# A fused attention and two-layer kernel on one core: the first group's attention with VectorE, ScalarE and GpSimd in program order

## The chip, the core and the metric

The kernel runs on one core of a Trainium2 chip. The time is device microseconds of that core for one execution of the whole program. In the rows, PE is TensorE (PEld its weight loads), DVE is VectorE, ACT is ScalarE, POOL is GpSimd and SP is the engine that issues nearly all transfers.

## What is computed

Block-causal attention over 4 batches, 8 heads, 576 tokens of 64 numbers, then two feed-forward layers on the 2304 token rows. Cut to what matters:

```
scores = (q @ k^T) / 8, keys of later 64-blocks masked
attn   = exp(scores - max) ; attn /= sum(attn) + 1e-9
x      = attn @ v                      # 2304 x 512
h = x @ w_in ; x = (h - tanh(h)) @ w_out                 # 512 -> 2048 -> 512
xn = x / rms(x) * g ; out = (silu(xn @ w_gate) * (xn @ w_val)) @ w_out2
```

All inputs are float32 (float64 words for the weights, which the kernel reads as pairs of 32-bit words and converts itself).

## The kernel before

**Tiling.** Attention runs over units: a unit is one batch with either its first 384 queries or its last 192. Four pairs of heads make one unit. The units in turn fill six groups of 384 token rows, and group g of the first layer (`w_in`, `tanh`, `w_out`) runs on TensorE while the attention of later groups is done beside it. The first group (batch 0, queries 0 to 383) has nothing to run beside: until its attention is done, TensorE has only attention work. This is the stretch from 8 to 41 us, and the change touches nothing else. Six score tiles belong to a pair in it, with 64, 128, 192, 256, 320 and 384 keys; the first three are called the first half here, the other three the second half. P1 to P4 are the pairs of the first group, P5 and P6 the first two of the second.

**One pair.** Its keys and queries are transposed on TensorE (L235; L242 from P5 on), and copied out of PSUM: keys by ScalarE to `kh`, queries by VectorE to `qf` in two copies of 64 partitions (of P1 the second is ScalarE's). Each score tile is a product on TensorE (L481), which VectorE reads out while it finds the row's extreme (L494), and ScalarE turns into exponentials with their sum (L496). GpSimd clears the padding (L499). After a half, ScalarE adds 1e-9 to the three sums (L504, tile `stat`), VectorE takes the reciprocals (L505), and GpSimd scales the three tiles by them (L510). TensorE then transposes the scaled tiles (L525); the six transposes are copied to `pp`, in this group 1, 3, 4 and 6 by VectorE (copy 1, 3, 4, 6 below), 2 and 5 by ScalarE. Twelve products with the values (L577) end the pair; ScalarE rounds the result to `xh` and VectorE subtracts to `xl`.

**The order on TensorE** is written out: `plan` lists scores ("s"), transposes ("t") and the product with the values ("a") by half-pairs, so that a half's transposes come two halves after its scores, and the "a" of a pair stands between the first-half scores and the first-half transposes of later pairs. So while the scores of P3 are read, P2's tiles are transposed and P1's values are multiplied. All score, transpose and product tiles of this stretch use eight PSUM banks in turn.

**Weight conversions.** `conv_upto` spreads four conversions of weight blocks over the first group. One takes two ScalarE passes over the loaded words (`cv`, `cu`), then two VectorE steps that clamp and join them (L144, L145); where the block is also split in two parts, a ScalarE rounding (`w<-cv`) and a VectorE subtraction follow. Conversions 1 and 3 (`w_in` blocks) are split, 2 and 4 are not.

**The order on the others.** Only TensorE's order is that of the program (L592). On VectorE, ScalarE and GpSimd the framework's scheduler places the instructions by its own estimate of times; each engine then runs its list in that order and waits at an instruction until its inputs are there.

## Time and profile before

| | us |
|---|---|
| median of 3 runs (lowest, highest) | 1019.18 (1018.07, 1019.55) |
| profiled execution | 1019.15 |
| its span, first to last instruction | 1017.4 |
| PE busy in the span | 1001.5 |
| DVE, ACT, POOL busy in the span | 704.4, 660.2, 347.4 |
| 8.00 to 41.04 us (first group's attention): PE, DVE, ACT, POOL busy | 31.56, 29.72, 27.77, 19.32 of 33.04 |
| 41.04 to 60.00 us: PE, DVE, ACT, POOL busy | 18.33, 16.19, 17.76, 7.12 of 18.96 |
| 60.00 to 120.00 us: PE, DVE, ACT, POOL busy | 58.83, 44.48, 50.35, 11.11 of 60.00 |

The 1.75 us between span and execution lie outside the instructions. Busy times of PE are modelled ends of pipelined products, so small gaps hide in them; starts of neighbouring rows tell more. For an engine that runs its list in order, the time from one row's start to the next row's start is what a row costs it.

### The profile page before, as it was taken

The page shows a single profiled execution, that of the slowest core. Times are in us where ns is not written, and L with a number is a line of the kernel's source. Part 1 is how long each engine was busy: PE and PEld are TensorE (multiplying, and loading weights), DVE is VectorE, ACT ScalarE, POOL GpSimd, SP SyncE. Part 2 cuts the span into 40 slices and gives each one's busy share as a digit, 9 for nine tenths or more (in the row PEclk, how much of TensorE's full clock was granted, in tenths as well). Part 3 has the DMA queues.
Part 4 walks back from the last instruction along what each step waited for, and adds up shares of the span by engine and source line. Part 5 has one row for each costly group of instructions (what it writes and reads, how often), then busy time and mean ns, then how long its engine had stood idle before and what let it go on. Part 6 is the DMA issues. An engine that isn't in the chain of part 4 may idle for free.

```text
span 1017.4 us, 17824 instructions
## 1 busy us (share of the span) xinstructions
PE 1001.5 (98%) x5983; PEld 921.6 (91%) x5983; DVE 704.4 (69%) x1497; ACT 660.2 (65%) x1530; POOL 347.4 (34%) x474
## 2 busy tenths in 40 slices
PE   8999999999999999999999999899999999999998
PEld 5766789999999999999899889899999999999998
DVE  6877867876777677787757887866854558644465
ACT  6978978887888777787857775635732247412253
POOL 6522112322233342434334425575121470112610
PEclk9999999999999999999999999999999999999999
DMA  9899959965798689867879997986796757876664
GB/s 236 250 342 340 283 173 258 272 205 140 197 254 206 187 248 271 234 215 240 279 225 377 363 364 299 322 336 265 284 333 256 252 224 265 303 270 239 248 235 139
DMA packets 185419, 265.22 MB, mean 261 GB/s; under 512 B 109040, under 2 KB 150384, under 8 KB 178032
## 3 DMA queue, kind: packets, MB, share of 16 engines
q1 hardware_dynamic: 184384, 263.83, 79.2%
q8 instruction: 47, 0.77, 0.3%
q10 hardware_dynamic: 944, 0.26, 0.1%
q14 instruction: 44, 0.36, 0.1%
HBM read 201.65 MB, written 62.39 MB: 260 GB/s over the span
## 4 chain that ended last, share of the span: by engine, by line
PE 80%; DVE 5%; ACT 4%; issue 1%; POOL 1%; DVEq 0%; ACTq 0%; POOLq 0%
PE gv L1064 5%; PE t L715 5%; PE t L481 5%; PE gv L1062 5%; PE gv L1063 5%; PE t L717 5%; PE t L716 5%; PE acc L748 5%; PE acc L750 5%; PE acc L749 4%; PE t L525 3%; PE ga L1064 3%; PE ga L1063 3%; PE ga L1062 3%; PE ga L748 3%; PE ga L750 2%
## 5 line engine op out<-in xcount | busy, mean ns | idle before, releaser
L715 PE MATMUL t<-xh,w 128*128 128x384 f32 x384 | 138.6, 361 | 0.1
L717 PE MATMUL t<-xh,w 128*128 128x384 f32 x384 | 129.9, 338 | 0.4 <-DVE w L108 0.2
L716 PE MATMUL t<-xl,w 128*128 128x384 f32 x384 | 129.2, 337 | 0.0
L1064 PE MATMUL gv<-xh,ws 128*128 128x384 f32 x322 | 108.5, 337 | 3.6 <-DVE ws L108 3.6
L1062 PE MATMUL gv<-xh,ws 128*128 128x384 f32 x322 | 108.3, 336 | 0.2 <-DVE vb L1115 0.2
L1063 PE MATMUL gv<-xl,ws 128*128 128x384 f32 x322 | 108.0, 336 | 0.0
L748 PE MATMUL acc<-w,gh 128*128 128x512 f32 x252 | 102.5, 407 | 0.0
L750 PE MATMUL acc<-w,gl 128*128 128x512 f32 x252 | 99.6, 395 | 0.4 <-DVE gl L108 0.3
L749 PE MATMUL acc<-w,gh 128*128 128x512 f32 x252 | 99.1, 393 | 0.0
L1119 POOL TENSOR_TENSOR g<-va,vb 128x384 f32<-128x384 f32 x36 | 40.5, 1126 | 150.9 <-ACT va L1118 150.9
L496 ACT ACTIVATE pt<-pt,stat 128x64 f32<-128x64 f32 (+2 forms) x144 | 80.0, 556 | 18.6 <-DVE pt L494 17.1
L494 DVE TENSOR_SCALAR_CACHE_REDUCE pt<-t 128x64 f32<-128x64 f32 (+2 forms) x144 | 63.8, 449 | 18.6 <-PE t L481 17.4
L715 PEld LDWEIGHTS t<-xh,w 128*128 128x128 f32 x384 | 72.3, 188 | 4.3 <-issue 1.5
L716 PEld LDWEIGHTS t<-xl,w 128*128 128x128 f32 x384 | 72.5, 189 | 2.3 <-issue 0.5
L717 PEld LDWEIGHTS t<-xh,w 128*128 128x128 f32 x384 | 72.1, 188 | 1.0 <-DVE w L108 1.0
L108 DVE TENSOR_TENSOR gl<-gt,gh 128x384 fp32r<-128x384 f32 x84 | 57.2, 681 | 16.4 <-ACT gh L103 16.1
L980 DVE TENSOR_TENSOR gt<-t,gt 128x384 f32<-128x384 f32 x84 | 46.2, 550 | 31.0 <-ACT gt L974 30.7
L108 DVE TENSOR_TENSOR pp<-t,pp 128x512 fp32r<-128x512 f32 (+3 forms) x112 | 55.3, 507 | 15.6 <-ACT pp L103 14.7
L525 PE MATMUL t<-ident,pt 128*128 128x128 f32 x400 | 64.4, 274 | 0.8 <-POOL pt L510 0.7
L1064 PEld LDWEIGHTS gv<-xh,ws 128*128 128x128 f32 x322 | 60.5, 188 | 4.5 <-DVE ws L108 4.5
L103 ACT ACTIVATE pp<-t 128x512 fp32r<-128x512 f32 (+5 forms) x144 | 60.2, 433 | 6.2 <-PE t L525 5.6
L525 PEld LDWEIGHTS t<-ident,pt 128*128 128x128 f32 x400 | 49.7, 140 | 14.1 <-issue 3.4
(188 smaller groups left out, 2960.0 us busy)
## 6 DMA issues: line engine op xcount, KB each, us to landing
ws<-w2d SPq DMA_DIRECT2D x26, 1792.0 KB, 7.9
ws<-wod SPq DMA_DIRECT2D x21, 1536.0 KB, 6.1
w<-w1d_i SPq DMA_DIRECT2D x60, 512.0 KB, 5.1
w<-w1d_o SPq DMA_DIRECT2D x48, 512.0 KB, 5.1
w2d<-ws SPq DMA_DIRECT2D x10, 1792.0 KB, 8.4
st<-in_moe_w_out SPq DMA_DIRECT2D x28, 512.0 KB, 5.9
st<-in_moe_w_in SPq DMA_DIRECT2D x16, 512.0 KB, 6.0
w1d_i<-w SPq DMA_DIRECT2D x16, 512.0 KB, 6.2
```

The lines of the kernel that those rows point to most:

```text
L108: eng.tensor_tensor(out=o, in0=full, in1=hi.bitcast(F32), op=ALU.subtract)
L496: ACT.activation(out=pt[:, 0:keys], in_=pt[:, 0:keys], func=AF.Exp, scale=-1.0, bias=least, accum_out=st[:, 8 + ti:9 + ti])
L525: PE.transpose(t[:, (j - a) * 128:(j - a + 1) * 128], pt[:, j * 128:(j + 1) * 128], ident)
L715: PE.matmul(h, lhsT=wh[:, c], rhs=xh[:, kk], start=(kk == 0), stop=False)
L716: PE.matmul(h, lhsT=wh[:, c], rhs=xl[:, kk], start=False, stop=False)
L717: PE.matmul(h, lhsT=wl[:, c], rhs=xh[:, kk], start=False, stop=(kk == KD - 1))
L748: PE.matmul(acc, lhsT=gh[:, c], rhs=wh, start=first, stop=False, skip_group_check=more)
L749: PE.matmul(acc, lhsT=gh[:, c], rhs=wl, start=False, stop=False, skip_group_check=more)
L750: PE.matmul(acc, lhsT=gl[:, c], rhs=wh, start=False, stop=last, skip_group_check=more)
L1062: PE.matmul(ps, lhsT=wh[:, c], rhs=xh[:, kk], start=(first and kk == 0), stop=False, skip_group_check=more)
L1063: PE.matmul(ps, lhsT=wh[:, c], rhs=xl[:, kk], start=False, stop=False, skip_group_check=more)
L1064: PE.matmul(ps, lhsT=wl[:, c], rhs=xh[:, kk], start=False, stop=(last and kk == nk - 1), skip_group_check=more)
```

## The change

For the first group alone, VectorE, ScalarE and GpSimd are put in the order in which the program is written, too, and the writing is changed to suit:

- The sums' addition, the reciprocals and the scaling (`norm`) are issued two steps of the list after their half's last score, not at once.
- A weight conversion is issued in four steps: the two ScalarE passes at once, clamp and join two steps later, rounding three, subtraction four steps later; the store of the block follows the last.
- The GpSimd reorders of P5's to P8's keys and queries (`kt`, `qt`) are issued behind the first half's scores of the pair two ahead of them.
- In the list itself all three transposes of a second half now stand behind all three scores (before, the first of them stood ahead of the third score).
- P1's two query copies, one on VectorE and one on ScalarE, are declared independent.

The core of the diff:

```diff
@@ q1, the query copies @@
-            for hh in range(2):
-                rnd(DVE if u.light and (hh == 0 or u.group or p) else ACT, diag(d["q"][0], hh, TG), part(ps, hh, TG))
+            engs = (DVE, DVE if u.group or p else ACT) if u.light else (ACT, ACT)
+            copies = [rnd(engs[hh], diag(d["q"][0], hh, TG), part(ps, hh, TG)) for hh in range(2)]
+            if engs[0] is not engs[1]:
+                tc.declare_no_dep(copies[1].ins, copies[0].ins, reason="they write different partitions")
@@ convert @@
-        pin(DVE.tensor_scalar(f, f, HIGHEST * REBIAS, -HIGHEST * REBIAS * NEGATIVE, ALU.min, ALU.max))
-        DVE.scalar_tensor_tensor(h.bitcast(I32) if l is None else t, t, 3, u, ALU.logical_shift_left, ALU.bitwise_or)
-        if l is None:
-            return
-        rnd(ACT, h, f)
-        lo(DVE, l, f, h)
+
+        def join():
+            pin(DVE.tensor_scalar(f, f, HIGHEST * REBIAS, -HIGHEST * REBIAS * NEGATIVE, ALU.min, ALU.max))
+            DVE.scalar_tensor_tensor(h.bitcast(I32) if l is None else t, t, 3, u, ALU.logical_shift_left, ALU.bitwise_or)
+        defer(2, join)
+        if l is not None:
+            defer(3, lambda: rnd(ACT, h, f))
+            defer(4, lambda: lo(DVE, l, f, h))
@@ plan @@
-                if av and self.pairs[av[0][1]][0].group == 0:
+                if any(self.pairs[e[0][1]][0].group == 0 for e in (av, tr) if e):
                     self.seq += sc + av + tr
@@ Attn @@
+        def defer(self, n, f):
+
+            if self.inorder:
+                self.waiting.append([n, f])
+            else:
+                f()
...
         def step(self):
+            self.tick()
@@ scores @@
             if ti % 3 < 2:
                 return
+            if self.inorder and ti == 2 and i + 2 in self.loads:
+                rows_in_turn(self.pairs[i + 2][0], self.loads[i + 2])
+            self.defer(2, lambda: self.norm(u, d, ti))
+
+        def norm(self, u, d, ti):
+            st = d["st"]
             r = st[:, 16 + ti - 2:17 + ti]
             ACT.activation(out=r, in_=st[:, 8 + ti - 2:9 + ti], func=AF.Copy, bias=1e-9)
             DVE.reciprocal(r, r)
@@ convert1 @@
-                convert(staged.pop(n), t[:, 0:512], t[:, 512:1024])
+                convert(staged.pop(n), t[:, 0:512], t[:, 512:1024], att.defer)
...
-                    SP.dma_start(out=w1d[0][j], in_=t.bitcast(F32))
+                    att.defer(4, lambda: SP.dma_start(out=w1d[0][j], in_=t.bitcast(F32)))
@@ around the first group's loop @@
+        inorder = ExitStack()
+        inorder.enter_context(tc.manual_schedule(engines={DVE.engine, ACT.engine, POOL.engine}))
+        att.inorder = True
...
+        att.tick(True)
+        att.inorder = False
+        inorder.close()
```

`tick`, called at the head of every step, counts the waiting pieces down and issues those that are due.

What this makes of the engines' lists is shown at three places. The names are those of the code: `pt` with a number of columns is a score tile read out (VectorE) or turned into exponentials (ScalarE), `pp` a copied transpose, `qf` the query copies.

VectorE (DVE), from the third score of P4 to the fourth, before:

```order
L494 TENSOR_SCALAR pt,stat<-t 128x192
L144 TENSOR_SCALAR cv<-cv 128x512
L505 RECIPROCAL stat<-stat 128x3
L145 SCALAR_TENSOR_TENSOR w_485<-cv,cu 128x512
L105 COPY pp<-t 128x2x64
L105 COPY pp<-t 128x2x2x64
```

and now:

```order
L145 TENSOR_SCALAR cv<-cv 128x512
L146 SCALAR_TENSOR_TENSOR w_487<-cv,cu 128x512
L523 TENSOR_SCALAR pt,stat<-t 128x192
L107 TENSOR_TENSOR xl<-t,xh 128x384
L540 RECIPROCAL stat<-stat 128x3
L104 COPY pp<-t 128x2x64
L104 COPY pp<-t 128x2x2x64
```

The join of a conversion stands ahead of the 192-key score, and the subtraction `xl` and its reciprocal ahead of the copies and of the 256-key score; before, they stood behind that score.

VectorE, next in the list: the second half of P4 and the start of P5, before:

```order
L494 TENSOR_SCALAR pt,stat<-t 128x256
L108 TENSOR_TENSOR xl<-t,xh 128x384
L505 RECIPROCAL stat<-stat 128x3
L494 TENSOR_SCALAR pt,stat<-t 128x320
L105 COPY pp<-t 128x2x2x64
L494 TENSOR_SCALAR pt,stat<-t 128x384
L105 COPY pp<-t 128x3x2x64
L494 TENSOR_SCALAR pt,stat<-t 128x64
L494 TENSOR_SCALAR pt,stat<-t 128x128
L105 COPY qf_139<-t 64x6x64 x2
L505 RECIPROCAL stat<-stat 128x3
```

and now:

```order
L523 TENSOR_SCALAR pt,stat<-t 128x256
L523 TENSOR_SCALAR pt,stat<-t 128x320
L523 TENSOR_SCALAR pt,stat<-t 128x384
L104 COPY pp<-t 128x2x2x64
L540 RECIPROCAL stat<-stat 128x3
L104 COPY pp<-t 128x3x2x64
L523 TENSOR_SCALAR pt,stat<-t 128x64
L523 TENSOR_SCALAR pt,stat<-t 128x128
L104 COPY qf_139<-t 64x6x64 x2
L523 TENSOR_SCALAR pt,stat<-t 128x192
```

The second half's reciprocal stood behind P5's query copies; it now stands directly behind copy 4 and ahead of copy 6 and of all of P5's rows.

ScalarE (ACT), from P5's 128-key exponentials to its 256-key ones, before:

```order
L496 ACTIVATE pt,stat<-pt,stat 128x128
L496 ACTIVATE pt,stat<-pt,stat 128x192
L103 ACTIVATE xh<-t 128x384
L504 ACTIVATE stat<-stat 128x3
L141 ACTIVATE cv<-st 128x512
L143 ACTIVATE cu<-st 128x512
L103 ACTIVATE pp<-t 128x2x64
L496 ACTIVATE pt,stat<-pt,stat 128x256
```

and now:

```order
L525 ACTIVATE pt,stat<-pt,stat 128x128
L525 ACTIVATE pt,stat<-pt,stat 128x192
L140 ACTIVATE cv<-st 128x512
L142 ACTIVATE cu<-st 128x512
L103 ACTIVATE xh<-t 128x384
L539 ACTIVATE stat<-stat 128x3
L103 ACTIVATE w_615<-cv 128x512
L103 ACTIVATE pp<-t 128x2x64
L525 ACTIVATE pt,stat<-pt,stat 128x256
```

The two passes of conversion 3 stand ahead of `xh`, and the rounding `w` ahead of the 256-key exponentials; before, the passes stood behind `xh` and the rounding two rows behind those exponentials.

On GpSimd the two reorders of a pair stand behind the scaling of a second half instead of ahead of it. On SP the store of the first converted block goes ahead of one query load. Behind the first group the lists of all engines are nearly those of before.

## Rows read from the trace of the kernel before

**Rows 1.** windows, to the first group's end: length, busy us (instructions) of each engine, PEclk, DMA, GB/s

```profile
8.00:41.04 33.04, 31.56 (x213) 23.16 (x213) 29.72 (x115) 27.77 (x102) 19.32 (x49) 1.00 1.02 246
```

**Rows 2.** waits, first 50 us: engine, tile, line <- releaser: us in total, times, longest

```profile
PEld t L525 <- POOL pt L510: 3.0, 5, 1.0
```

**Rows 3.** timeline, PE: start, duration (us), line, operation, count [idle before <-releaser]

```profile
8.02 1.44 PE L481 MATMUL t<-kh,qf 128*128 128x64 f32 x8 [0.60 <-ACT qf L103]
...
30.12 0.33 PE L481 MATMUL t<-kh,qf 128*128 128x64 f32 x2
...
36.09 0.33 PE L481 MATMUL t<-kh,qf 128*128 128x64 f32 x2
...
37.81 0.44 PE L715 MATMUL t<-xh,w 128*128 128x384 f32 x1
...
39.59 1.52 PE L577 MATMUL t<-pp,vn 128*64 128x384 f32 x12
```

**Rows 4.** timeline, ACT, 0 to 75 us: first pair's second query copy

```profile
7.39 0.48 ACT L103 ACTIVATE qf<-t 64x384 f32<-64x384 f32 x1 [0.58 <-DVE qf L105]
```

**Rows 5.** timeline, DVE, 0 to 75 us: a reciprocal, then the fourth pair

```profile
15.63 0.18 DVE L505 RECIPROCAL stat<-stat 128x3 f32<-128x3 f32 x1 [0.52 <-ACT stat L504]
...
24.75 0.55 DVE L105 COPY pp<-t 128x384 f32<-128x384 f32 x1
25.22 0.20 DVE L494 TENSOR_SCALAR_CACHE_REDUCE pt<-t 128x64 f32<-128x64 f32 x1
...
26.71 0.36 DVE L494 TENSOR_SCALAR_CACHE_REDUCE pt<-t 128x192 f32<-128x192 f32 x1
...
27.45 0.69 DVE L145 SCALAR_TENSOR_TENSOR w<-cv,cu 128x512 int32<-128x512 int32 x1
28.07 0.61 DVE L105 COPY pp<-t 128x128 f32<-128x128 f32 x2
28.60 0.41 DVE L494 TENSOR_SCALAR_CACHE_REDUCE pt<-t 128x256 f32<-128x256 f32 x1
...
28.94 0.55 DVE L108 TENSOR_TENSOR xl<-t,xh 128x384 fp32r<-128x384 f32 x1
29.41 0.16 DVE L505 RECIPROCAL stat<-stat 128x3 f32<-128x3 f32 x1
29.49 0.46 DVE L494 TENSOR_SCALAR_CACHE_REDUCE pt<-t 128x320 f32<-128x320 f32 x1
```

**Rows 6.** timeline of all engines, 39.9 to 42.0 us: hand-overs between DVE and ACT

```profile
40.02 0.36 DVE L494 TENSOR_SCALAR_CACHE_REDUCE pt<-t 128x192 f32<-128x192 f32 x1
...
40.42 0.45 ACT L496 ACTIVATE pt<-pt,stat 128x192 f32<-128x192 f32 x1 [0.88 <-DVE pt L494]
...
40.99 0.20 ACT L504 ACTIVATE stat<-stat 128x3 f32<-128x3 f32 x1
...
41.16 0.49 ACT L103 ACTIVATE xh<-t 128x384 fp32r<-128x384 f32 x1
41.23 0.18 DVE L505 RECIPROCAL stat<-stat 128x3 f32<-128x3 f32 x1 [0.76 <-ACT stat L504]
...
41.68 0.56 DVE L108 TENSOR_TENSOR xl<-t,xh 128x384 fp32r<-128x384 f32 x1 [0.28 <-ACT xh L103]
```

**Rows 7.** timeline, ACT, 0 to 75 us: fourth pair

```profile
25.47 0.47 ACT L103 ACTIVATE kh<-t 128x384 f32<-128x384 f32 x1
25.84 0.67 ACT L141 ACTIVATE cv<-st 128x512 f32<-128x512 f32 x1
...
27.06 0.34 ACT L496 ACTIVATE pt<-pt,stat 128x64 f32<-128x64 f32 x1
...
29.05 0.51 ACT L496 ACTIVATE pt<-pt,stat 128x256 f32<-128x256 f32 x1
...
29.99 0.56 ACT L496 ACTIVATE pt<-pt,stat 128x320 f32<-128x320 f32 x1 [0.34 <-DVE pt L494]
...
30.92 0.60 ACT L496 ACTIVATE pt<-pt,stat 128x384 f32<-128x384 f32 x1
```

More of the change, by code (lines that the diff above doesn't have):

```diff
@@ L102, in rnd @@
         if eng is ACT:
-            ACT.activation(out=o, in_=i, func=AF.Copy)
-        else:
-            eng.tensor_copy(out=o, in_=i)
+            return ACT.activation(out=o, in_=i, func=AF.Copy)
+        return eng.tensor_copy(out=o, in_=i)
     def lo(eng, o, full, hi):
@@ L131, in stage, with convert @@
         return st
-    def convert(st, h, l=None):
+    def convert(st, h, l=None, defer=lambda n, f: f()):
         e = st.rearrange("p (e t) -> p e t", t=2)
@@ L291, in kq_loads, with rows_in_turn @@
         return d
+    def rows_in_turn(u, d):
+        if by_rows(u) and "kt" not in d:
+            d["kt"] = reorder("kt", d["kr"], POOL)
+            d["qt"] = reorder("qt", d["qr"], POOL)
     def v_loads(u, p, d):
         b, W = u.b, u.nk
-        if by_rows(u):
-            d["kt"] = reorder("kt", d["kr"], POOL)
-            d["qt"] = reorder("qt", d["qr"], POOL)
+        rows_in_turn(u, d)
         if u.group == 0:
@@ L364, in __init__ @@
             self.ready = set()
+            self.inorder = False
+            self.waiting = []
         def plan(self, units):
@@ L450, in prep, with tick @@
                     self.load()
+        def defer(self, n, f):
[3 more added lines that the diff above has]
+                f()
+        def tick(self, end=False):
+            while self.waiting:
+                now = []
+                for w in self.waiting:
+                    w[0] -= 1
+                    if w[0] <= 0 or end:
+                        now.append(w)
+                self.waiting = [w for w in self.waiting if w not in now]
+                for w in now:
+                    w[1]()
+                if not end:
+                    return
         def step(self):
+            self.tick()
             kind, i, t = self.seq[self.pos]
@@ L660, in convert1 @@
             o = t[:, 512 * (j % 2):512 * (j % 2) + 512]
-            convert(staged.pop(n), o)
+            convert(staged.pop(n), o, None, att.defer)
             wo[j] = o
             if j % 2:
-                SP.dma_start(out=w1f[j // 2], in_=t)
+                att.defer(2, lambda: SP.dma_start(out=w1f[j // 2], in_=t))
         fstaged = {}
```

## The prediction

> **What bounds the kernel now.** I read the busy times by stretch first. Between 8.00 and 41.04 us, the first group's attention, PE is busy for 31.56 of 33.04 us and DVE for 29.72 [rows 1]: TensorE has some 1.5 us without work there, VectorE 3.3 us. The granted clock is 1.00. So two engines are close to full, and neither has much to give. Next, the waits: TensorE's weight loads wait 3.0 us in the first 50 us for GpSimd's scaled tiles [rows 2]. That is what a change here can aim at. Then TensorE's timeline: from P5's first score to P6's first score is 30.12 to 36.09 us [rows 3], and TensorE works without a mark of idle time in these rows. I take 5.97 us as its own need for a pair. Last, VectorE's rows of P4 [rows 5]: they follow each other start to start, with a conversion between them, because the scheduler put ready work wherever a result of ScalarE was not yet there. The one wait among the rows shown, 0.52 us before the reciprocal at 15.63, is the kind of place to watch: VectorE waits there for the sums.
>
> What counts for the new order is therefore not how much each engine has to do, which hardly changes, but which row waits at the head of VectorE's list while ready rows stand behind it.
>
> **The change part by part.**
>
> *Query copies of P1.* ScalarE's copy sat idle 0.58 us for VectorE's [rows 4], and TensorE 0.60 us for ScalarE's copy (8.02, [rows 3]). Without the dependence both go at once. I take 0.5 us gained, bounds 0 and 0.6: everything up to P2 hangs on that first score.
>
> *Transposes behind the third score, reorders behind the scaling.* These take TensorE's waits for GpSimd away; at most the 3.0 us of [rows 2], as long as VectorE and ScalarE keep up. The reorders on GpSimd are wanted a pair later, and the query load on SP that now stands behind a store is wanted later still, so I cost both at nothing. If that cover were gone, the price would be a wait of TensorE at the transposes of P5.
>
> *Reciprocals.* They are called deferred, and in the program they are. In VectorE's list they have come forward, though: the scheduler had the second half's behind the next pair's query copies, and it now stands between copies 4 and 6. Likewise `xl` now stands ahead of the copies and of the 256-key score. VectorE runs its list in order, so I follow one round of it, from a 64-key score (0) to the next pair's, without a conversion:
>
> - The 64-key, 128-key and two query rows cost 26.71 − 25.22 = 1.49 us [rows 5]: the 192-key score starts at 1.49.
> - Its exponentials start 0.40 later (40.02 to 40.42), last 0.45, then `xh`, and `xl` starts 0.52 after `xh` (41.16 to 41.68) [rows 6]: `xl` starts at 2.86. TensorE's product is done by then.
> - `xl` 0.47 (28.94 to 29.41), reciprocal 0.08 (to 29.49), copies 1 and 3 together 0.53 (28.07 to 28.60; the row merges them) [rows 5]: the 256-key score starts at 3.94.
> - Its exponentials start 0.45 later (28.60 [rows 5] to 29.05 [rows 7]); the three of the half take 0.51, 0.56 and 0.60 [rows 7]; then the sums, and the reciprocal starts 0.24 after these (40.99 to 41.23 [rows 6]): it starts at 6.30. VectorE's other rows up to it are long done.
> - Reciprocal 0.08, copy 6 0.47 (24.75 to 25.22 [rows 5]): 6.85 us.
>
> Nothing in this round can overlap: it goes VectorE, ScalarE, VectorE, ScalarE, VectorE. It takes 6.85 us where TensorE needs 5.97, so VectorE and ScalarE set the pace, each waiting for the other twice a pair. TensorE is late from then on, so its own gain above is not seen.
>
> *Conversions.* A ScalarE row hands on 0.03 to 0.05 us after its end [rows 6], and the next starts about 0.1 before that end (`kh` 0.47, next start 0.37 later [rows 7]). So a conversion pass, 0.67 long [rows 7], is handed on 0.70 after its start, and the second pass starts 0.57 after the first. The join's last step costs VectorE 0.62 (27.45 to 28.07 [rows 5]); the first I take as 0.47, like copy 6. The closing subtraction has 512 columns against 384 of `xl`: an estimate of 0.47 × 4/3 = 0.63. I take the rounding like a pass.
>
> - Conversion 1, in P3's round. VectorE starts P2's 256-key score at 15.63 + 0.08 + 0.33 = 16.04, as ScalarE's sums of P2's first half are no earlier than before; the reciprocal comes 2.36 later, at 18.40, copy 6 at 18.48 and, without a conversion, P3's 64-key score at 18.95. The passes stand behind the sums (18.16) and copy 5 (18.26, 0.37): they start at 18.63 and 19.20, the join ends at 19.90 + 0.62, and the 64-key score starts at 20.52: +1.57. The rounding stands behind the 64-key exponentials and `kh`, so the subtraction starts 0.25 + 0.33 + 0.37 + 0.70 = 1.65 after the 64-key score, and the 192-key score at 2.28 and not 1.49: +0.79. Together +2.36.
> - Conversion 2, in P4's round: the passes start 0.95 and 1.52 after the 64-key score, the join ends at 2.22 + 0.62 = 2.84, where the 192-key score would have stood at 1.49: +1.35.
> - Conversion 3, in P5's round: the passes stand ahead of `xh`, so `xl` starts 1.14 later, at 4.00. Behind its reciprocal come the join (4.55 to 5.64), the rounding, handed on at about 6.4, the subtraction (to 7.03) and copy 3: the 256-key score starts at 7.36 and not 3.94: +3.42.
>
> *The sum.* Copy 6 of the round starts at 18.48, 18.48 + 9.21 = 27.69, + 8.20 = 35.89, + 10.27 = 46.16. In P6 TensorE then has to read 64 to 192 keys' scores and nine products of the first layer before P4's product with the values. The 192-key score needs the bank of P5's 384-key score, which VectorE has read by about 45.1 (estimate: 64-key score at 36.36, 256-key at +7.36, two more rows of 0.4 and one of 0.55); 0.3 for the score, 39.59 − 37.81 = 1.78 for the nine products [rows 3] give 47.1, later than copy 6 allows. Before it was 39.59 [rows 3]: +7.5, less 0.5 from the start, +7.0 us. Behind the first group the lists are nearly the same, and PE has hardly an idle moment to take the loss back, so it stays. Against the profiled execution's own time: 1019.15 + 7.0 = 1026.15, and 1019.15 is within 0.03 of the median. **I forecast 1026.2 us.**
>
> The bounds: if a conversion costs only VectorE's own rows (1.09 for the join, 0.63 for the subtraction), the three cost 1.72 + 1.09 + 1.72 = 4.5 and not 7.1, and the time is 1023.6. If each of some ten hand-overs of the three rounds is 0.1 slower, and the 0.5 at the start is not gained, it is 1027.7.
>
> **The rivals.**
>
> - *The round is not closed* (0.09). TensorE's own 5.97 us would hide the waits if VectorE ran far behind TensorE anyway, so that only the conversions add up: 7.5 − 3 × 0.88 = 4.9, less 0.5, or less still with the cheap conversions: 1021.3 to 1023.6. For it: eight PSUM banks let VectorE lag. Against it: no row of TensorE but `xl`'s stands in the round.
> - *Faster* (0.04). The waits for GpSimd go and nothing replaces them: up to 3.0 + 0.5 us, 1015.7 to 1017.1. One thing decides: VectorE's new waits must stay below what it idles now, 3.3 us over five pairs or 0.66 a pair. I work out 1.37 − 0.36 = 1.0 at `xl` alone (the 192-key row lasts 0.36 [rows 6]).
> - *Within 0.2%* (0.07), 1017.1 to 1021.2: gains at the start and at GpSimd are eaten by waits a third as long as mine; or the lists on the chip hardly differ in effect. The shown lists speak against it.
> - *TensorE's clock falls* (0.05). With rounds of 8 to 10 us around 5.97 us of work TensorE stands still for over a microsecond before each product with the values. If it fell from 2.4 to 1.2 GHz, a pair would take 11.9 us (twice [rows 3]), more than my rounds of 9.2, 8.2 and 10.3: up to 8.0 us more, 1029 to 1034. Against it: the granted clock stays 1.00 in a stretch that has idle gaps too [rows 1], if shorter ones. The Trainium skill bears on this, in "TensorE: Matmul & The Clock Gate", section "HAM oscillation — how this bites in real kernels": gaps in TensorE's work can drop its clock to half, and pauses for operands then cost twice. No run here shows it yet.
>
> **How the numbers follow.** Forecast 0.75, with 1023.6 to 1027.7 as its own range; the others as given. 0.2%, or 2.0 us, is about what a measurement of this kernel can tell from no change. Slower: 0.75 + 0.09 + 0.05 = 0.89; same 0.07; faster 0.04. The range goes from 1022.0, which takes in most of the first rival, to 1028.5; it leaves out the faster and equal cases, the clock and the tails of the forecast, some 0.18.
>
> **What would show it.** In the changed trace VectorE's reciprocal of a second half should show idle time of about 0.8 us before it, ended by ScalarE's sums, in every pair; `xl` some 1 us ended by `xh`. The reciprocal-to-reciprocal rounds should be 9.2, 8.2 and 10.3 us, TensorE should wait for VectorE's copy before each product with the values, and no longer for GpSimd. P1's first score should start near 7.5. P4's product with the values should start near 46.6 and everything after it keep that distance of 7 us. I am wrong if VectorE's waits before these rows are short, if TensorE's 5.97 us still sets the pace, or if the loss is made good between 50 and 120 us.

## The result and the profile after

The changed kernel takes 1028.91 us (median of 4 runs, 1027.22 to 1032.46), the kernel before 1019.12 in the same comparison: a ratio of 1.0099, 95% interval 1.0073 to 1.0125. The forecast was 1026.2, its range 1022.0 to 1028.5. The sign and the mechanism came out as worked out, the size did not: +9.8 us and not +7.0, and the median lies 0.4 us above the range. The profiled execution took 1029.75 us, its span is 1028.0 (+10.6).

The windows of the changed kernel, columns as in [rows 1]:

```profile
8.00:41.04 33.04, 26.85 (x168) 18.71 (x166) 23.90 (x90) 23.73 (x84) 15.42 (x42) 1.00 0.83 201
41.04:60.00 18.96, 15.77 (x83) 12.23 (x84) 13.32 (x42) 13.17 (x39) 6.96 (x15) 0.91 0.58 177
60.00:120.00 60.00, 58.94 (x284) 40.88 (x283) 45.57 (x106) 50.59 (x122) 13.41 (x30) 1.00 1.03 344
```

VectorE, 29.72 us busy in the first of these stretches before [rows 1], is busy for 23.90; TensorE fell from 31.56 to 26.85. No engine is full any more: they wait for each other. From 60 us on all is as before.

VectorE's timeline from P3 to P6 (start, duration in us, line, operation, and the idle time before with what ended it):

```profile
17.94 0.18 DVE L540 RECIPROCAL stat<-stat 128x3 f32<-128x3 f32 x1 [0.82 <-ACT stat L539]
18.03 0.53 DVE L104 COPY pp<-t 128x384 f32<-128x384 f32 x1
18.88 0.60 DVE L145 TENSOR_SCALAR cv<-cv 128x512 f32<-128x512 f32 x1 [0.32 <-ACT cv L140]
19.59 0.87 DVE L146 SCALAR_TENSOR_TENSOR cv<-cv,cu 128x512 int32<-128x512 int32 x1
20.38 0.21 DVE L523 TENSOR_SCALAR_CACHE_REDUCE pt<-t 128x64 f32<-128x64 f32 x1
...
23.96 0.56 DVE L107 TENSOR_TENSOR xl<-t,xh 128x384 fp32r<-128x384 f32 x1 [0.99 <-ACT xh L103]
...
27.50 0.18 DVE L540 RECIPROCAL stat<-stat 128x3 f32<-128x3 f32 x1 [0.82 <-ACT stat L539]
...
36.25 0.18 DVE L540 RECIPROCAL stat<-stat 128x3 f32<-128x3 f32 x1 [0.82 <-ACT stat L539]
...
40.76 0.56 DVE L107 TENSOR_TENSOR xl<-t,xh 128x384 fp32r<-128x384 f32 x1 [2.11 <-ACT xh L103]
...
46.56 0.18 DVE L540 RECIPROCAL stat<-stat 128x3 f32<-128x3 f32 x1 [0.82 <-ACT stat L539]
```

This is the round of the prediction, row by row: 0.82 us for the sums before every second-half reciprocal from P2 on (P1's, at 13.32, waits 0.47), 0.99 us (2.11 with conversion 3's passes ahead) for `xh` before `xl`. In [rows 5] `xl` and the reciprocal behind it (28.94 and 29.41) stood without idle time, as the scheduler had put other rows ahead of them.

TensorE's timeline; the rows answer to [rows 3]:

```profile
7.20 1.44 PE L510 MATMUL t<-kh,qf 128*128 128x64 f32 x8 [0.16 <-ACT qf L103]
...
36.98 1.52 PE L612 MATMUL t<-pp,vn 128*64 128x384 f32 x12 [1.23 <-ACT pp L103]
...
45.45 0.59 PE L510 MATMUL t<-kh,qf 128*128 128x192 f32 x2
46.96 0.69 PE L750 MATMUL t<-xh,w 128*128 128x384 f32 x1 [0.91 <-ACT pp L103]
...
49.68 0.52 PE L752 MATMUL t<-xh,w 128*128 128x384 f32 x1
50.13 1.52 PE L612 MATMUL t<-pp,vn 128*64 128x384 f32 x12
```

P4's product with the values starts at 50.13, before at 39.59 [rows 3]: 10.54 us later, and the span is 10.6 us longer. The nine first-layer products ahead of it took 50.13 − 46.96 = 3.17 us, before 1.78. The windows of that place tell why (last columns: PEclk, DMA, GB/s):

```profile
46.00:47.00 1.00, 0.09 (x2) 0.05 (x1) 0.44 (x2) 0.87 (x4) 0.17 (x1) 0.83 0.08 21
47.00:48.00 1.00, 1.00 (x3) 1.00 (x4) 0.99 (x6) 0.65 (x3) 1.00 (x3) 0.50 0.00 0
48.00:49.00 1.00, 1.00 (x4) 1.00 (x4) 0.93 (x3) 0.56 (x4) 1.00 (x4) 0.50 0.00 0
49.00:50.00 1.00, 1.00 (x4) 0.69 (x3) 0.00 (x0) 0.55 (x2) 0.65 (x2) 0.50 0.00 0
```

The granted clock fell to half, 1.2 GHz, for just these products, and was back at 0.96 in the microsecond after.

### The profile page after: what moved, and what is told of

Read it like the earlier page. It is cut to its first block, busy times and chain, and to the rows that moved or that the text cites. A ratio compares the mean times of both kernels' runs of the same rounds, so it can differ in the third digit from the quotient of the medians.

```text
span 1028.0 us, 17838 instructions
## 1 busy us (share of the span) xinstructions
PE 1004.9 (98%) x5983; PEld 923.2 (90%) x5983; DVE 705.4 (69%) x1497; ACT 661.3 (64%) x1530; POOL 346.7 (34%) x474
## 4 chain that ended last, share of the span: by engine, by line
PE 78%; DVE 4%; ACT 4%; DMA 2%; issue 1%; POOL 1%; SPq 0%; DVEq 0%; ACTq 0%; POOLq 0%
PE t L510 5%; PE t L750 5%; PE t L752 5%; PE t L751 5%; PE gv L1105 5%; PE gv L1103 5%; PE gv L1104 5%; PE acc L789 4%; PE acc L791 4%; PE acc L790 4%; PE t L560 3%; PE ga L1105 3%; PE ga L1103 3%; PE ga L1104 3%; PE ga L789 2%; PE ga L791 2%
```

## The experiments

Every kernel is compared with the kernel before on the same chip (its medians there are 1019.02 to 1019.75). Three columns, from the profiled execution of each, tell where a difference lies: the start of P1's first score, the start of P4's product with the values (39.59 before, 50.13 changed), and the time from there to the end of the span. The first score's place varies from 6.48 to 8.02 us, also between kernels whose start is the same (8.02 before, 7.08 in e15_before_b), so differences of up to 1.5 us in P4's place can come from the start. The last column turned out to matter: it has two values, 977 to 979 us and 974 to 976, by the order that the scheduler writes for VectorE in the second layer.

| kernel | us (median) | ratio, 95% interval | first score | P4's product | from there to the end |
|---|---|---|---|---|---|
| before (its profile) | 1019.1 | | 8.02 | 39.59 | 977.8 |
| changed | 1028.91 | 1.0073 to 1.0125 | 7.20 | 50.13 | 977.9 |
| e1_sched | 1019.80 | 0.9997 to 1.0025 | 7.45 | 39.94 | 978.4 |
| e2_recip | 1032.59 | 1.0119 to 1.0149 | 6.74 | 53.92 | 977.1 |
| e6_all | 1030.65 | 1.0104 to 1.0134 | 7.65 | 50.63 | 977.7 |
| e3_xl | 1028.40 | 1.0070 to 1.0104 | 7.62 | 51.02 | 975.9 |
| e4_conv | 1027.72 | 1.0062 to 1.0092 | 6.48 | 48.05 | 978.0 |
| e8_split | 1025.52 | 1.0041 to 1.0071 | 6.52 | 45.79 | 978.4 |
| e11_split_xl | 1022.71 | 1.0012 to 1.0040 | 7.25 | 43.57 | 977.6 |
| e13_split_conv | 1025.77 | 1.0034 to 1.0078 | 7.47 | 44.36 | 978.6 |
| e9_both | 1016.92 | 0.9959 to 0.9983 | 6.70 | 40.72 | 974.2 |
| e12_conv9 | 1017.18 | 0.9955 to 0.9981 | 6.90 | 40.85 | 975.6 |
| e5_fill | 1025.58 | 1.0050 to 1.0084 | 6.80 | 49.67 | 974.1 |
| e14_fill_a | 1030.63 | 1.0077 to 1.0114 | 6.98 | 51.51 | 977.6 |
| e15_before_b | 1017.92 | 0.9964 to 0.9985 | 7.08 | 41.81 | 975.9 |
| e16_copy5 | 1025.47 | 1.0030 to 1.0061 | 6.67 | 48.96 | 975.0 |
| e10_front | 1021.34 | 0.9996 to 1.0028 | 7.51 | 41.33 | 978.3 |

The theory is that of the prediction: in program order VectorE and ScalarE form a closed round, and each wait at the head of VectorE's list is paid by all.

### Is it the program order? (e1_sched)

```diff
-        inorder.enter_context(tc.manual_schedule(engines={DVE.engine, ACT.engine, POOL.engine}))
-        att.inorder = True
```

> The changed kernel with the three engines' lists left to the scheduler again in the first group; the list of steps on TensorE, the early third score and the independent query copies stay. If the lists in program order are the cause, the loss is gone: 1017.0 to 1019.5 us, P4's product with the values starts near 39 us as before (39.59) and not at 50.1. If the moved transposes or the query copies are the cause, it stays above 1024 us.

1019.80 us, 0.3 above the range expected, and the interval of the ratio includes no change; P4's product at 39.94. Nearly the whole loss is gone, though the new place of the transposes and the independent query copies stay. The deferred steps work only with the program order and go with it. So the program order, with its rows where the changed kernel puts them, makes the loss.

### Which place? (e2_recip, e6_all, e3_xl, e4_conv)

e2_recip defers the whole `norm`; e3_xl defers `xl` alone, e4_conv spreads the conversions' steps wider; e6_all does all three (left out here: the stores of converted blocks move back along with the conversions' steps):

```diff
-            self.defer(2, lambda: self.norm(u, d, ti))
+            self.defer(6, lambda: self.norm(u, d, ti))
...
-            lo(DVE, xl[:, p, u.off:u.off + nq], o[:, 0:nq], hv)
+            self.defer(4, lambda: lo(DVE, xl[:, p, u.off:u.off + nq], o[:, 0:nq], hv))
...
-        defer(2, join)
+        defer(4, join)
...
-            defer(3, lambda: rnd(ACT, h, f))
-            defer(4, lambda: lo(DVE, l, f, h))
+            defer(5, lambda: rnd(ACT, h, f))
+            defer(7, lambda: lo(DVE, l, f, h))
```

> The changed kernel with sums, reciprocals and scaling issued six steps after their half, not two, so that VectorE's reciprocals stand some four rows further back. If VectorE's waits for ScalarE's sums (0.82 us in each of four second halves) are part of the loss, these waits are gone and VectorE's rounds are 0.8 us shorter: 3 to 4 us less than the changed kernel, 1024 to 1026 us. If the rounds are set by something else (the conversions, xl), the time stays within 1 us of the changed kernel's 1028.9.

> The changed kernel with all suspected waits moved back in VectorE's list, still in program order: reciprocals six steps after their half, xl four steps after the product, a conversion's join four, rounding five and subtraction seven steps after its passes. If the places of these rows are the loss, it is nearly all gone: 1017.5 to 1020 us, VectorE's rounds 6 to 7.5 us. If program order itself costs wherever the rows stand, it stays above 1023 us.

Both missed: 1032.59 and 1030.65 us, above the changed kernel. VectorE's timeline of e2_recip, and a wait of TensorE's weight loads in its first 52 us:

```profile
28.72 0.18 DVE L540 RECIPROCAL stat<-stat 128x3 f32<-128x3 f32 x1 [0.76 <-ACT stat L539]
```

```profile
PEld t L560 <- POOL pt L545: 5.1, 5, 2.6
```

The wait before the reciprocal did not go. `norm` holds the ScalarE sums too, and these moved along, behind the next pair's first exponentials; the reciprocal meets them as late as before, only further down. The scaling behind it came later as well, and TensorE's weight loads wait 5.1 us for GpSimd, 1.8 in the changed kernel, 3.0 before [rows 2]. The granted clock fell to 0.50 too (in e2_recip from 15 to 18 and 49 to 55 us, in e6_all from 28 to 34 and 48 to 51), so both times hold a price of the clock that no run separates. To move the consumer one should not move its producer: e9_both below, which differs from e6_all in leaving the sums' additions in place and the reciprocals about one step less far back, has P4's product 9.9 us earlier.

> One part alone: the subtraction to xl stands four steps later in VectorE's list (behind the copies of the first-half transposes), all else as in the changed kernel. Theory A (VectorE and ScalarE pace each other: each wait at the head of VectorE's list is paid in full): the waits of 0.99, 0.99 and 2.11 us before xl fall below 0.3 us each; the other wait, 0.82 us before the second-half reciprocals, stays; 2 to 4 us less than the changed kernel, 1025 to 1027, and P4's product with the values starts at 46 to 48 us and not at 50.1. Theory B (TensorE's copies for the product with the values and its clock set the time, the wait at xl is cover): within 1 us of 1029 and the product at 49.5 to 50.5.

1028.40 us, and P4's product later, at 51.02 (0.9 us, or 0.5 counted from the first score): theory A as it was put here missed. VectorE's timeline of e3_xl, the first-half reciprocals of P3 to P5:

```profile
24.48 0.18 DVE L540 RECIPROCAL stat<-stat 128x3 f32<-128x3 f32 x1 [1.08 <-ACT stat L539]
...
33.34 0.18 DVE L540 RECIPROCAL stat<-stat 128x3 f32<-128x3 f32 x1 [1.08 <-ACT stat L539]
...
41.48 0.18 DVE L540 RECIPROCAL stat<-stat 128x3 f32<-128x3 f32 x1 [2.20 <-ACT stat L539]
```

The waits of 0.99, 0.99 and 2.11 us before `xl` became waits of 1.08, 1.08 and 2.20 before the next row of the list: its sums stand behind `xh` on ScalarE. Moving the row that shows the wait is not enough when the row behind it needs the same engine at the same point.

> One part alone: the steps of a conversion stand four, five and seven steps behind its two passes and not two, three and four, so that clamp, join and subtraction find their inputs ready. The rows themselves stay. Theory A: only their own waits go (0.32, 0.23 and 0.49 us) and the 2.11 us at xl shrink little, since the passes stay where they are in ScalarE's list: 0.5 to 1.5 us less, 1027 to 1028.5. Theory C (the conversions' place costs most of the loss): 3 us or more less, below 1026.

1027.72 us, within theory A's numbers: the conversions' own waits go, the waits at `xl` ahead of P4's product stay (1.51, 1.59 and 2.10 us). Their place alone is a small part: P4's product comes 2.1 us earlier, 0.7 of which is the earlier start.

### Sums early, reciprocal late (e8_split, e11_split_xl, e13_split_conv, e9_both, e12_conv9)

```diff
             ACT.activation(out=r, in_=st[:, 8 + ti - 2:9 + ti], func=AF.Copy, bias=1e-9)
-            DVE.reciprocal(r, r)
+            self.defer(3 if d is not self.loads.get(0) else 1, lambda: self.scale(u, d, ti, r))
+
+        def scale(self, u, d, ti, r):
+            st = d["st"]
+            DVE.reciprocal(r, r)
```

This is e8_split. e11_split_xl adds the deferred `xl` of e3_xl, e13_split_conv the steps of e4_conv, e9_both both; e12_conv9 is e9_both with the closing subtraction nine steps behind the passes.

> The ScalarE sums stay where the changed kernel has them; only the reciprocal and the GpSimd scaling behind them are issued three steps later (one step for P1), so that the second-half reciprocal stands behind copy 6 and the next 64-key score. Theory A: the 0.82 us of idle time before the second-half reciprocals goes in each of four rounds, rounds shorten by 0.6 to 0.9 us, TensorE's gaps before the products with the values shrink: 1024 to 1026.5, P4's product at 46 to 48 us. Theory D (deferring the scaling makes TensorE wait for GpSimd again, as in the kernels with the whole group deferred by six steps): 1029 or more, with over 2 us of TensorE waiting for GpSimd before 50 us.

> Two of the three parts: reciprocal and scaling three steps after the sums, xl four steps later; conversions as in the changed kernel. If the parts add up (reciprocal alone gave -3.4 us, xl alone -0.5): 1025. If they are heads of one closed round, which opens only when every one of its waits is gone (theory A in a stricter form): 1019 to 1023, with conversions' own waits of 0.2 to 1.2 us left, P4's product with the values at 41 to 45 us.

> The other two of the three parts: reciprocal and scaling three steps after the sums, conversions in steps of four, five and seven; xl stays where the changed kernel has it. If the parts add up (-3.4 and -1.2 us): 1024.3. If every wait of one closed round must be gone: VectorE still waits 1 to 3 us at each xl, so near the sum, 1023 to 1025.5, while the pair with xl comes out lower.

> The three edits together (reciprocal and scaling three steps after the sums, xl four steps later, conversions in steps of four, five and seven), still all three engines in program order. Theory A: no row at the head of VectorE's list waits more than 0.4 us; TensorE's own 5.97 us per pair sets the pace again, its clock holds at 1.00: 1018 to 1021, P4's product at 39 to 42 us. If it stays above 1024, a fixed order loses by something other than these three places.

e8_split: 1025.52 us, P4's product at 45.79, about as theory A has it (46 to 48). VectorE's waits in its first 52 us, then the same two in the changed kernel:

```profile
DVE xl L107 <- ACT xh L103: 6.9, 4, 2.8
...
DVE stat L544 <- ACT stat L539: 0.7, 3, 0.2
```

```profile
DVE stat L540 <- ACT stat L539: 4.5, 6, 0.8
DVE xl L107 <- ACT xh L103: 4.1, 3, 2.1
```

The wait for the sums is nearly gone, 4.3 us of P4's lag with it (0.7 of which is the earlier start), and the waits at `xl` are what is left: 0.99, 0.99 and 2.13 us ahead of P4's product, as in the changed kernel; the longest, 2.8, is P4's own behind it. The pair with `xl` (e11) gives 1022.71 and 43.57, the pair with the conversions (e13) 1025.77 and 44.36, all three (e9) 1016.92 and 40.72. At P4's product, where the second layer plays no part, `xl` alone is worth −0.9 us (it is later), the conversions 2.1, the reciprocals 4.3, which adds up to 5.5; together they bring 9.4.

Two other things stand in these differences, and neither makes the parts add. Counted from the first score it is −0.5, 1.4 and 3.7, together 4.6, against 8.9. About 1.4 of the 8.9 are the clock: the nine products ahead of P4's took 3.17 us in the changed kernel, 3.26, 3.03 and 2.82 in e3, e4 and e8, but 1.77 to 1.78 in e11, e13 and e9, whose granted clock stayed at 1.00. Among those three, taking out the last wait brings more than taking it out alone: from e13 to e9 `xl` is worth 2.9 (alone −0.5), from e11 to e9 the conversions 2.3 (alone 1.4). The parts don't add: while one kind of wait is left, much of the loss stays, which is the direction of the theory's stricter form.

For e13 the times can't tell (1025.77, above both numbers expected, with 1024.12 to 1027.58 in its runs); its P4 is 1.4 us earlier than e8's (2.4 counted from the first score), at a clock that did not fall, and its waits at `xl` are 7.2 us in all (1.9 of it behind P4's product), as they must be while `xl` stays.

VectorE's waits of e9_both in the first 52 us, and its TensorE row for P4:

```profile
DVE xl L107 <- ACT xh L103: 1.9, 1, 1.9
DVE w L107 <- ACT w L103: 0.9, 1, 0.9
...
DVE stat L544 <- ACT stat L539: 0.4, 2, 0.2
```

```profile
40.72 1.51 PE L616 MATMUL t<-pp,vn 128*64 128x384 f32 x12
```

The expectation that no row waits more than 0.4 us missed with the 0.9 at `w`; the 1.9 at `xl` is P4's own, at 42.81, behind its product. So program order can come within 1.1 us of the scheduler's list in this stretch (2.5 counted from the first score). It doesn't beat it there. The 2.8 us by which e9_both beats the kernel before must lie elsewhere.

> As the kernel with all three edits, but the closing subtraction of a conversion nine steps behind the passes and not seven: the 0.93 us that VectorE waited for ScalarE's rounding at 20.47 goes. VectorE's list at 640 to 660 us, where TensorE waited 4.6 us for converted weights before and 1.4 us in the kernel with three edits, is the one of that kernel. Theory: first group 0 to 1 us shorter, 1016 to 1017; its lead over before comes from 640 to 660 us and not from the first group.

1017.18 us, 0.2 above the range expected, P4's product at 40.85: the 0.93 us wait was no part of the path, or was replaced (0.6 us of it are left). The order of the second layer is that of e9_both, and so is the time.

### Where the faster kernels gain (e5_fill, e14_fill_a, e15_before_b)

e5_fill and e14_fill_a repeat score products of P5's second half and P6's first half to keep TensorE busy; each repeat writes the same tile again:

```diff
+                for _ in range({(4, 3): 3, (4, 4): 3, (4, 5): 3, (5, 0): 3, (5, 1): 3, (5, 2): 3}.get((i, ti), 0)
+                               if self.inorder and n == len(terms) - 1 else 0):
+                    PE.matmul(s[:, 0:z - a], lhsT=q[0][:, ti].rearrange("p h c -> p (h c)"), rhs=kh[:, a:z],
+                              start=True, stop=True)
```

(e14_fill_a; e5_fill has two extra in P5 and three in P6.)

> The changed kernel with the score products of P5's second half issued three times and of P6's first half four times, each time from zero, so that TensorE has some 5 us more to do in its gaps from 38 to 47 us, none of it waited for. If the lower clock from 46 to 50 us costs, the granted clock stays 1.000, the nine first-layer products take 1.8 and not 3.2 us, and all times lie at 1027 to 1028 us with little spread. If the clock is not what makes the changed kernel's times spread from 1027.2 to 1032.5, the extra products change nothing or cost up to 2 us.

1025.58 us, 3.3 less than the changed kernel, with a granted clock of 1.00 from 5 to 60 us and the nine products in 1.8 us: outside both expectations. That looked like the price of the clock. But P4's product stands at 49.67, only 0.5 earlier; the rest lies behind it. TensorE's waits from 600 to 700 us, the first two rows of each, in the kernel before, the changed one, and e5_fill:

```profile
PE gv L1064 <- DVE ws L108: 3.6, 3, 1.3
PE ga L1064 <- DVE ws L108: 1.0, 1, 1.0
```

```profile
PE gv L1105 <- DVE ws L107: 3.6, 3, 1.3
PE ga L1105 <- DVE ws L107: 1.0, 1, 1.0
```

```profile
PE gv L1109 <- DVE ws L107: 1.4, 2, 1.0
PE ga L1107 <- DVE vb L1160: 0.3, 1, 0.3
```

Behind the first group the framework's scheduler writes the lists, and a different first group can tip it into another order hundreds of microseconds later. In the one, a conversion's second join stands ahead of the subtractions to `ws` that TensorE waits for, in the other behind them. So a kernel with other numbers of repeats follows, which keeps the order of before and changed:

> The changed kernel with every score product of P5's second half and P6's first half issued four times (three extra, results unchanged), so that TensorE's gaps between 38 and 47 us are filled; VectorE's list behind 600 us is that of the changed kernel, which was not so in the first kernel with extra products (there TensorE waited 1.4 us for converted weights at 640 to 680 us and not 4.6). If TensorE's clock costs the changed kernel what its own runs say (1027.2 and 1028.1 at a granted clock of 1.000, 1029.8 at 0.998, 1032.5 at 0.994): 1027 to 1028.5 in every run, the nine products in 1.8 us. If it cost 3 us or more: 1024 to 1026.

1030.63 us with a granted clock of 0.999 to 1.000 in every run and P4's product at 51.51. That is above both expectations: three repeats each keep TensorE busy for all of 40 to 55 us, so the filling itself became the path. What it does show is that a full clock alone doesn't bring 1025; e5_fill owed that to the second layer. The clock's price is read from the changed kernel's own runs instead, below.

e15_before_b is the kernel before with three repeats of P7's 192-key product, which tip the scheduler into the other order:

```diff
+                for _ in range({(6, 2): 3}.get((i, ti), 0) if n == len(terms) - 1 else 0):
+                    PE.matmul(s[:, 0:z - a], lhsT=q[0][:, ti].rearrange("p h c -> p (h c)"), rhs=kh[:, a:z],
+                              start=True, stop=True)
```

> The kernel before with three repeated score products (192 keys, P7), which leave the first group's lists as before but make the scheduler write VectorE's list behind 640 us as in the kernel with all three edits. If that list is where the kernel with three edits gains on the kernel before: 2 to 3 us less than before, 1016.5 to 1018, with TensorE's waits for converted weights 1.4 us and not 4.6. If the gain is the first group's: within 0.5 us of before or above it.

1017.92 us, 1.8 less than before, although it does more. Windows of 640 to 680 us, of the kernel before and of e15_before_b:

```profile
640.00:680.00 40.00, 35.46 (x197) 34.17 (x198) 31.51 (x49) 20.52 (x34) 27.66 (x27) 1.00 0.90 322
```

```profile
640.00:680.00 40.00, 38.46 (x218) 37.51 (x217) 33.75 (x52) 20.36 (x34) 26.84 (x27) 1.00 0.88 319
```

TensorE does 3.0 us more work in the same 40 us. Two products of TensorE that start at 630.02 and 680.10 us in the kernel before, 50.1 apart, are 49.9 apart in the changed kernel, and 46.5 in e15_before_b, e9_both and e12_conv9 (at full clock in all of them). 1.0 to 1.6 of these 3.6 us are lost ahead of this place, between 500 and 630 us, so that the whole gains 2 to 3. That is where e9_both and e12_conv9 gain too (38.48 and 38.42 us busy there): they beat both kernels, and not in the stretch that was changed. The profiled execution of e15_before_b, with P4's product at 41.81, is the slowest of its twelve (1019.57): a transfer came late in it, as in e10_front below.

### What delays the nine products? (e16_copy5)

```diff
-            self.defer(2, lambda: self.norm(u, d, ti))
+            self.defer(2 if ti == 2 else 3, lambda: self.norm(u, d, ti))
...
-                    rnd(ACT if u.group or ti % 3 == 1 else DVE, hv[:, a:z].bitcast(F32), tv)
+                    rnd(ACT if u.group or ti == 1 else DVE, hv[:, a:z].bitcast(F32), tv)
```

> The changed kernel with copy 5 on VectorE, between copy 4 and the reciprocal, where VectorE is idle for 0.82 us; the sums and the reciprocal one step later, their place among the rest unchanged. If copy 5 behind ScalarE's sums is what the nine first-layer products wait for in P6: they start 0.5 to 0.9 us earlier against P6's 192-key score, with no wait over 0.4 us ahead of them; P4's product at 48 to 49.5 us. If it is something else: a wait of 0.9 us stays there. VectorE's list behind 640 us is the other one here, so that up to 2.7 us of a lower time come from there: the place of P4's product decides.

ScalarE's timeline of the changed kernel (the second row is copy 5), then VectorE's (copies 4 and 5) and TensorE's of e16_copy5:

```profile
46.32 0.21 ACT L539 ACTIVATE stat<-stat 128x3 f32<-128x3 f32 x1
46.43 0.47 ACT L103 ACTIVATE pp<-t 128x384 f32<-128x384 f32 x1
```

```profile
45.29 0.89 DVE L104 COPY pp<-t 128x256 f32<-128x256 f32 x2
```

```profile
45.71 0.90 PE L510 MATMUL t<-kh,qf 128*128 128x192 f32 x2
46.23 0.70 PE L750 MATMUL t<-xh,w 128*128 128x384 f32 x1
...
48.96 1.52 PE L612 MATMUL t<-pp,vn 128*64 128x384 f32 x12
```

From the 192-key score to the first of the nine products it is 0.52 us, in the changed kernel 46.96 − 45.45 = 1.51, of which 0.91 are shown as a wait for copy 5. In both kernels the first of the nine starts just behind the end of copy 5 (46.43 + 0.47 = 46.90, then 46.96; 45.29 + 0.89 = 46.18, then 46.23). The marked wait is gone, and P4's product starts 1.2 us earlier, 0.6 counted from the first score; the clock fell here too (0.50 from 45 to 48 us), and the nine products took 2.73 us. So the products wait for copy 5, which stood behind the sums on ScalarE. They don't read its result; they need a PSUM bank. By the code their tile is taken from the pool of five banks (`tpp`), out of the turn of the eight, and the oldest tile there is the one that copy 5 reads. The time, 1025.47 us, contains the other order of the second layer.

### The start (e10_front)

The scheduler's lists and TensorE's old list; of the change only the independent copies stay.

> The scheduler's lists on all three engines, the list of TensorE as before; of the change only P1's independent query copies (and the reorders' place in the text) stay. P1's first score 0.5 to 0.8 us earlier, as in the changed kernel. If the gain at the start lasts: 1018.3 to 1019.0 where before has 1019.1 to 1019.7. If the first group does not wait for its start, as it has VectorE as a second full engine: within 0.3 us of before.

1021.34 us, where before has 1019.62 on this chip; the interval of the ratio includes no change. Neither expectation fits: the first score came earlier (7.51, 8.02 before [rows 3]), P4's product later (41.33). GpSimd's timeline in the kernel before, in e10_front and in e15_before_b:

```profile
19.30 0.61 POOL L229 COPY kt<-kr 96x512 f32<-96x512 f32 x1 [2.04 <-DMA kr<-in_k]
```

```profile
20.86 0.66 POOL L230 COPY kt<-kr 96x512 f32<-96x512 f32 x1 [4.11 <-DMA kr<-in_k]
```

```profile
21.07 0.61 POOL L229 COPY kt<-kr 96x512 f32<-96x512 f32 x1 [4.74 <-DMA kr<-in_k]
```

and TensorE's in e10_front:

```profile
22.76 0.44 PE L560 MATMUL t<-ident,pt 128*128 128x128 f32 x2 [2.19 <-POOL pt L545]
```

The scheduler keeps the reorder ahead of the scaling, and GpSimd waits for the keys' transfer, which came 1.6 us later; TensorE waits behind it. The granted clock then falls to 0.50 from 24 to 27 us. Why the transfer came later is not settled. It isn't the edit alone: e15_before_b has the lists of the kernel before in its first group, with the old query copies, and its reorder starts later still. So e10_front doesn't tell what a gain at the start is worth; it shows that such a gain can be lost behind a late transfer.

## Why the prediction was right and wrong

**What bounds the kernel, and the round.** Right. The waits of 0.82 and 0.99 us, forecast as 0.8 and 1.0, stand in every round from P2's second half on (2.11 in P5's), and e8, e11 and e9 show that these and the conversions' waits are most of the loss: with them out of the way P4's lag falls from 10.5 to 1.1 us, some 1.4 of it because the clock no longer falls. One detail differs: the wait before each product with the values was forecast for VectorE's copy, and the profile's mark names ScalarE's (36.98, above).

**Query copies.** About as forecast: TensorE's wait ahead of the first score fell from 0.60 to 0.16 us, 0.44 against 0.5. The first score itself came 0.8 us earlier (7.20 against 8.02); the rest of that is the start of this execution, for the first query copy stands at 6.43, before at 6.80, and the first score of e15_before_b is at 7.08 with the old copies. The second-half reciprocal of P2 stands at 17.94, forecast 17.90; without the early start it would have been later, so that this fit is in part luck. That the gain counts for more than the first score was assumed; no run shows it.

**Conversions.** Reciprocal to reciprocal it is 27.50 − 17.94 = 9.56, 8.75 and 10.31 us, forecast 9.21, 8.20 and 10.27. The misses of 0.35 and 0.55 are the join: from its first row to the row behind it 20.38 − 18.88 = 1.50 us in P3's round and 31.36 − 29.73 = 1.63 in P4's, put at 0.47 + 0.62 = 1.09; rows that last 0.42 and 0.69 elsewhere last 0.60 and 0.87 here.

**The sum, the step that failed.** P4's product was worked out as 45.1 less 0.5 = 44.6 for the 192-key score, 0.3 and 1.78 us on: 46.7 (46.6 by its own rounding). Measured: 45.45 (+0.85, from the rounds, with a first score 0.3 earlier than forecast), then 1.51 and not 0.3 (+1.21), then 3.17 and not 1.78 (+1.39). The second term was missed: the prediction asked which bank the 192-key score needs, and not which one the nine products behind it need, copy 5's (e16); their tile doesn't follow the turn of the eight banks that is described for the other tiles. The third is TensorE's clock, taken from [rows 3] as if it must hold.

**The clock.** The rival at 0.05 came about, but in another place and not in every run. It was put before the products with the values; there TensorE stood for 1.24, 1.23 and 1.23 us at a granted clock of 1.00 between 15 and 40 us. It fell after 40 to 45 us, where TensorE was busy for 3.07 us in pieces with gaps of 0.55, 0.81 and 0.55, and the 0.91 at 46. The four runs took 1027.22 and 1028.07 us at a mean clock of 1.000, 1029.75 at 0.998 and 1032.46 at 0.994; by an estimate from the two runs at 1.000, without the fall the time would have been about 1027.6, within the range. The Trainium skill, "TensorE: Matmul & The Clock Gate", section "HAM oscillation — how this bites in real kernels", has gaps in TensorE's work drop the clock to half so that pauses for operands cost twice; the rows at 46 to 50 us agree in the fall (0.50, after gaps of at most 1.24 us), and the bank's wait was followed by 1.39 us of slow products.

**Waits for GpSimd.** They should have gone; 1.8 us of 3.0 [rows 2] are left; what they cost at the end no run shows.

**The rest keeps its distance.** Right: from P4's product to the end it is 977.9 us, before 977.8. That this is no law, but the luck of an unchanged order in the second layer, the prediction didn't see: 2 to 3 us hang on it.

## What to carry to other kernels

An engine that runs its list in order pays for every wait at its head; when two engines hand work back and forth, look for the closed round, and don't add up its waits one by one, for when one is taken out, the next row often waits for the same producer. To hide a hand-over, issue the producer at once and the consumer a few rows later; moved together they still meet. When a scheduler writes the rest of the program, compare runs at a landmark behind the change as well as at the end, or a change of order elsewhere will be booked to the wrong account; and count to the landmark from one at the start, which moved by up to 1.5 us here.

## What the runs showed of the hardware

VectorE's 512-column conversion rows and GpSimd's rows on SBUF slow each other where they overlap, and either can bear it. The join took 0.60 and 0.87 us beside a scaling and a reorder (at 18.88, above), and 0.40 and 0.69 later in the same kernel, where the scaling beside it was the slow one. VectorE and GpSimd of the changed kernel there, then GpSimd of e8_split with the same three tiles and no such row beside it:

```profile
41.32 0.40 DVE L145 TENSOR_SCALAR cv<-cv 128x512 f32<-128x512 f32 x1
41.75 0.69 DVE L146 SCALAR_TENSOR_TENSOR cv<-cv,cu 128x512 int32<-128x512 int32 x1
```

```profile
41.50 1.58 POOL L545 TENSOR_SCALAR pt<-pt,stat 128x64 f32<-128x64 f32 x3 [2.16 <-DVE stat L540]
```

```profile
31.28 1.06 POOL L549 TENSOR_SCALAR pt<-pt,stat 128x64 f32<-128x64 f32 x3 [2.18 <-DVE stat L544]
```

The Trainium skill has a rule for it, in "SBUF — State Buffer", section "SBUF: two separate sides": the two engines share one pair of ports, which one instruction (of VectorE's only some kinds, among them those with two inputs in SBUF) holds to its end while the other engine's waits. The rows at 41 us agree, with the longer time on GpSimd's side alone; at 18.88 both sides took longer (GpSimd's scaling 1.71 us, against 1.54 at 27.77 in the same kernel). That it is a lock and not a share of bandwidth they don't show. A price taken from one row holds for what ran beside it there.
